# Gate products ahead of the value products, and the third half's q and k cast by GpSimd, in a fused attention and ReGLU kernel

## The chip, the cores and the metric

One core of a Trainium2 chip. The metric is the device time of one launch in microseconds (us); "before" is the kernel as it was, "changed" the kernel with the change. Runs of one kernel lie within 0.1 to 0.8% of each other; a step of 2 us between runs of the changed kernel's relatives is taken up in experiment 7.

## The reference, cut to what matters

```python
# attention: 4 batches, 8 heads, 768 positions, head dimension 64
scores = scale * q @ k.T + bias          # keep 8 global keys and a window of 96
a = softmax(scores); attn = a @ v
x = attn.transpose(0, 2, 1, 3).reshape(3072, 512)
# feed-forward: d_model 512, d_ff 1536
out = (relu(x @ w_gate) * (x @ w_val)) @ w_out      # float32
```

The kernel works on eight "halves" of 384 positions, two to a batch. Half s has its q and k transposed (head dimension onto partitions), its scores, exponentials and weighted sums made, and then goes through the feed-forward. Work of several halves is woven into one program for each engine. "Third half" below is s = 2, the first of the second batch.

## The kernel before: the parts that matter

The loads of q and k. The first half comes as fp32 on SyncE's queue; the second and third are cast to bf16 by the DMA on GpSimd's queue, in four pieces each:

```python
    def load_qk_cast(s, parts=2):

        b, half = divmod(s, 2)
        n = H // parts
        for i, (src, name) in enumerate(((q, "qs"), (k, "ks"))):
            t = stage.tile([128, H, NN * D], FP32, name=name)
            qk16[s, i] = t.rearrange("p h x -> p (h x)").bitcast(BF16).rearrange(
                "p (h x) -> p h x", h=H)[:, :, 0 : NN * D]
        for h in range(0, H, n):
            for i, src in ((1, k), (0, q)):
                nc.gpsimd.dma_start(
                    out=qk16[s, i][:, h : h + n],
                    in_=src[b, h : h + n, half * QH : (half + 1) * QH, :].rearrange(
                        "h (p n) d -> p h (n d)", n=NN))
```

The transposes on TensorE, and VectorE's copies out of PSUM, where the results of the matmuls lie. The DMA-cast halves are stored head by head, so each head has its own transpose of 64 columns:

```python
    def piece_t(s, p, pool=av_psum, name="av_ps"):
        tp = pool.tile([128, 512], FP32, name=name)
        tp = tp[:, 0:QH].bitcast(BF16).rearrange("d (i t) -> d i t", i=2)
        tp_of[s, p] = tp
        for i in (1, 0):
            for n in range(NN):
                for e in range(1 if s == 0 else 2):
                    r = slice(0, 128) if s == 0 else slice(64 * e, 64 * e + 64)
                    src = (cast_of[s, p][:, i, n] if s == 0
                           else qk16[s, i][:, 2 * p + e, n * D : (n + 1) * D])
                    nc.tensor.matmul(tp[r, i, n * 128 : (n + 1) * 128],
                                     lhsT=src, rhs=ident, is_transpose=True,
                                     start=(i == 1 and n == 0), stop=(i == 0 and n == NN - 1))

    def piece_copy(s, p):
        b, half = divmod(s, 2)
        tp = tp_of[s, p]
        put_keys(nc.vector.tensor_copy, nc.vector.tensor_copy, kT[b % 2][p], tp[:, 1, :], half)
        for e in range(2):
            r = slice(64 * e, 64 * e + 64)
            nc.vector.tensor_copy(qTb[s % 2][r, p, e, :], tp[r, 0, :])
```

The order of GpSimd's work and of the loads between the first and the third half. All of GpSimd's instructions and DMA issues run in this order:

```python
    for j in range(4, NT):
        load_v(0, j)
    load_w_group(1)
    load_w_group(2)
    load_qk_cast(2)
    load_w(wo_sb, moe_w_out, 0, DM)
# ... the second half and the first gate and value products ...
    for h in (0, 1, 6, 7):
        setup_mask(h)
    load_v_half(2)
    for p in range(HP):
        nc.gpsimd.memset(kT[1][p][:, 3, 32:128].bitcast(mybir.dt.uint32), 0)
        nc.gpsimd.memset(kT[1][p][:, 6, NG + 48 : 128].bitcast(mybir.dt.uint32), 0)
    nc.gpsimd.memset(vbuf[1][:, NT - 1, :].bitcast(mybir.dt.uint32), 0)
    for i in range(2):
        nc.gpsimd.memset(qz[i].rearrange("t n p e z -> t (n p e z)").bitcast(mybir.dt.uint32), 0)
    for j in range(NT):
        fill_ones(nc.gpsimd, 1, j)
    T2 = [(0.0, f) for p in range(HP) for f in (lambda p=p: piece_t(2, p, *QKB), lambda p=p: piece_copy(2, p))]
    weave(f1_1[G[0]] + f1_0[G[1]][4:] + f1_1[G[1]],
          [(0.05 + 0.06 * j, lambda j=j: fill_ones(nc.vector, 0, j)) for j in range(NT)],
          [(0.6, lambda: load_qk_after(3)), (0.6, lambda: load_v_half(3))],
          spread(T2, 0.55, 0.95))
```

`weave` places pieces of other work between the feed-forward products; `T2` is the list of the third half's transposes and copies, spread between 55% and 95% of that stretch.

`load_v_half(2)` puts three things in line: the load of the 8 global rows of v (GpSimd's queue), their spread to the other six v tiles of the batch by six small copies inside SBUF (SyncE's queue, which waits for that load), and the loads of four v tiles.

The softmax here doesn't subtract the row's maximum and nothing guards it: scores larger than these inputs give would overflow.

## Time and profile before

| | before |
|---|---|
| time, median | 253.31 us |
| span of the profiled run | 251.2 us |
| TensorE busy | 239.8 us (95%) |
| TensorE reaches the third half's transposes | 44.05 us |
| GpSimd's 13.78 us of idle time ends | 53.30 us |

TensorE is the bound. Times in timelines are from the span's start. A bracket at the end of a row is the idle time of that engine just before the row, and what ended it. PE is TensorE, DVE VectorE, ACT ScalarE, POOL GpSimd, SPq SyncE's queue, and L312 is line 312 of that kernel. qT and kT are the transposed q and k, xT is the attention's result transposed, ht the hidden values of the feed-forward. PEclk is the clock that TensorE was granted, as a share of full speed (in a page, in tenths). Only the stretch that the first part of the change aims at is shown here, from TensorE's timeline of the kernel before (start, length, line, operation):

```profile
19.41 0.34 PE L312 MATMUL qk_ps<-dd,sid 128*128 128x216 bf16 x2 [0.86 <-DVE qT L300]
...
20.27 0.36 PE L290 MATMUL ff_ps<-ident,ks 128*64 128x128 bf16 x6
```

The bias matmuls of the second half's first scores wait 0.86 us for VectorE's q copies.

### The profile page before, as it was taken

The numbers are of one execution on the slowest core, as the hardware profiler recorded it, in microseconds if no ns is written. First come the engines' busy times: TensorE is split into PE (matmuls) and PEld (weight loads), VectorE is DVE, ScalarE is ACT, GpSimd is POOL, SyncE is SP. The second block draws the span as 40 slices with busy tenths as digits, with TensorE's granted clock in tenths as the row PEclk, the third lists the DMA queues.
The fourth block names the chain that finished last, engine by engine and source line by source line (L and its number), as shares of the span: only waits on it lengthen the run. The fifth ranks groups of instructions, "written<-read, shape, count | busy, mean of one in ns | idle before, by whom it ended". The sixth has DMA issues, their size and how long they took to land.

```text
span 251.2 us, 4845 instructions
## 1 busy us (share of the span) xinstructions
PE 239.8 (95%) x1741; PEld 142.5 (57%) x1749; DVE 137.1 (55%) x352; ACT 156.8 (62%) x323; POOL 88.4 (35%) x205
## 2 busy tenths in 40 slices
PE   7679999999999999999999999999999999999993
PEld 4566665556454666556664666556655666556541
DVE  5959557966441467527662567527662557424410
ACT  7886874257654687557774687557774687553321
POOL 8996542059491067202527076203520000000000
PEclk9999999999999999999999999999999999999999
DMA  6999999959699666739468966738432100020012
GB/s 187 166 179 188 207 197 207 145 140 156 77 211 172 193 174 150 53 108 266 104 88 88 248 173 146 55 111 261 104 86 82 43 3 0 19 110 0 0 42 84
DMA packets 77431, 31.56 MB, mean 126 GB/s; under 512 B 57440, under 2 KB 74336, under 8 KB 77408
## 3 DMA queue, kind: packets, MB, share of 16 engines
q0 software_dynamic: 36080, 9.48, 37.1%
q1 hardware_dynamic: 41328, 21.78, 31.7%
q8 instruction: 13, 0.21, 0.4%
q14 instruction: 10, 0.08, 0.1%
HBM read 28.38 MB, written 6.29 MB: 138 GB/s over the span
## 4 chain that ended last, share of the span: by engine, by line
PE 83%; DVE 7%; ACT 6%; DMA 1%; issue 1%; SPq 1%; ACTq 0%
PE ff_ps L478 45%; PE ff_ps L501 24%; PE av_ps L410 5%; PE qk_ps L382 5%; DVE xT L427 2%; DMA qs<-in_q_dram 1%; DVE ht L494 1%; ACT es L335 1%; ACT grelu L487 1%; PE av_ps L441 1%; ACT rcp L424 1%; PE qk_ps L330 1%; ACT lnd L419 1%; DVE qT L300 1%; PE qk_ps L290 1%
## 5 line engine op out<-in xcount | busy, mean ns | idle before, releaser
L478 PE MATMUL ff_ps<-xT,wv 128*128 128x384 bf16 x384 | 78.1, 326 | 0.8 <-DVE ht L494 0.3
L478 PE MATMUL ff_ps<-xT,wg 128*128 128x384 bf16 x384 | 78.1, 326 | 0.0
L487 ACT ACTIVATE grelu<-ff_ps 128x384 bf16<-128x384 f32 x96 | 47.0, 490 | 33.7 <-PE ff_ps L478 13.5
L501 PE MATMUL ff_ps<-wo_sb,ht 128*128 128x512 bf16 x280 | 66.4, 379 | 0.4
L494 DVE TENSOR_TENSOR ht<-ff_ps,grelu 128x384 bf16<-128x384 f32 x96 | 53.2, 555 | 21.5 <-PE ff_ps L478 13.4
L427 DVE TENSOR_TENSOR xT<-av_ps,rcp 64x384 bf16<-64x384 f32 x48 | 26.6, 555 | 46.4 <-ACT rcp L424 41.9
L478 PEld LDWEIGHTS <-wv 128*128 128x128 bf16 x384 | 36.0, 97 | 23.4 <-issue 2.1
L478 PEld LDWEIGHTS <-wg 128*128 128x128 bf16 x384 | 36.0, 97 | 23.0 <-issue 0.2
L394 DVE TENSOR_TENSOR es<-es,m_all 128x432 bf16<-128x432 bf16 (+5 forms) x113 | 34.3, 332 | 26.0 <-ACT es L385 25.2
L385 ACT ACTIVATE es<-qk_ps 128x432 bf16<-128x432 f32 (+2 forms) x75 | 39.5, 529 | 9.4 <-PE qk_ps L382 7.7
L501 PEld LDWEIGHTS <-ht 128*128 128x128 bf16 x288 | 27.0, 97 | 28.3
L419 ACT ACTIVATE lnd<-av_ps 64x384 f32<-64x384 f32 x48 | 23.3, 485 | 13.3 <-PE av_ps L410 12.6
L506 ACT COPY osb<-ff_ps 128x512 f32<-128x512 f32 x24 | 14.1, 586 | 26.7 <-PE ff_ps L501 25.8
L338 POOL CAST kc<-ks 128x384 bf16<-128x384 f32 x20 | 10.0, 544 | 52.6 <-DMA ks<-in_k_dram 52.6
L382 PE MATMUL qk_ps<-qT,kT 128*128 128x432 bf16 (+5 forms) x113 | 25.8, 286 | 0.0
L151 POOL DMA_DIRECT2D vbuf<-in_v_dram x28 | 24.3, 874 | 3.8 <-DMA wg<-in_moe_w_gate_dram 2.4
L410 PEld LDWEIGHTS <-vbuf 128*128 128x128 bf16 x216 | 18.3, 98 | 8.7 <-issue 0.8
L410 PE MATMUL av_ps<-es,vbuf 128*128 128x216 bf16 (+4 forms) x216 | 21.4, 226 | 0.6 <-DVE xT L427 0.6
L382 PEld LDWEIGHTS <-kT 128*128 128x128 bf16 x113 | 10.9, 98 | 7.5
L346 POOL CAST qz<-qs 128x192 bf16<-128x192 f32 x40 | 12.4, 358 | 1.8 <-DMA qs<-in_q_dram 1.8
L424 ACT ACTIVATE rcp<-lnd 128x384 f32<-128x384 f32 x24 | 12.5, 523 | 0.8
L335 ACT ACTIVATE es<-qk_ps 128x432 bf16<-128x432 f32 (+2 forms) x15 | 7.0, 536 | 3.2 <-PE qk_ps L330 3.2
(92 smaller groups left out, 146.1 us busy)
## 6 DMA issues: line engine op xcount, KB each, us to landing
out_dram<-osb SPq DMA_DIRECT2D x24, 256.0 KB
ks<-in_k_dram SPq DMA_DIRECT2D x5, 768.0 KB
qs<-in_q_dram SPq DMA_DIRECT2D x5, 768.0 KB
vbuf<-in_v_dram POOLq DMA_DIRECT2D x24, 120.0 KB, 4.5
wg<-in_moe_w_gate_dram POOLq DMA_DIRECT2D x3, 512.0 KB, 9.1
wv<-in_moe_w_val_dram POOLq DMA_DIRECT2D x3, 512.0 KB, 10.9
wo_sb<-in_moe_w_out_dram POOLq DMA_DIRECT2D x1, 1536.0 KB, 19.1
ks<-in_k_dram SPq DMA_DIRECT2D x4, 192.0 KB
```

Source lines behind the costliest of these rows:

```text
L151: nc.gpsimd.dma_start(out=v_dst(b, NG + r0, NG + r0 + n, j), in_=v[b, :, KT * j + r0 : KT * j + r0 + n, :].rearrange("h p d -> p h d"))
L382: nc.tensor.matmul(ps[:, c : c + n_], lhsT=kt[:, j, :], rhs=qd[:, :, :, a : a + w], start=True, stop=True)
L385: nc.scalar.activation(es[:, 0:cols], ps[:, 0:cols], AF.Exp, bias=0.0, scale=scale)
L394: nc.vector.tensor_mul(e4, e4, mk)
L410: nc.tensor.matmul(av3[:, :, a : a + w], lhsT=vb[:, j, z0 : z0 + 128], rhs=es[:, c : c + NN * w].rearrange("k (n p) -> k n p", n=NN), star ...
L419: nc.scalar.activation(ln[o0 : o0 + 64], av[d0 : d0 + 64, 0:QH], AF.Ln, bias=0.0, scale=1.0)
L424: nc.scalar.activation(rc, ln, AF.Exp, bias=0.0, scale=-1.0)
L427: nc.vector.tensor_tensor(xT_of[s][r, p, :], av_of[s, p, e_][r, 0:QH], rc[r], op=ALU.mult)
L478: nc.tensor.matmul(st[key][:, 0:QH], lhsT=w_of(w, dc, fc), rhs=xT_of[c][:, dc, :], start=(dc == 0), stop=(dc == N_DC - 1))
L487: nc.scalar.activation(gr, psg[:, 0:QH], AF.Relu, bias=0.0, scale=1.0)
L494: nc.vector.tensor_tensor(ht[:, fc, :], psv[:, 0:QH], st["r", fc], op=ALU.mult)
L501: nc.tensor.matmul(ps2, lhsT=ht[:, fc, n * 128 : (n + 1) * 128], rhs=wo_sb[:, fc, :], start=(fc == 0), stop=(fc == N_FC - 1))
```

## The change

Its intent, as far as the diff shows it: (1) bring the first gate weights in before the second q/k half of the second half, and use them at once, so that TensorE has products to do while attention is short of work; (2) bring the third half's q and k in as fp32, let GpSimd cast them into the paired layout, and transpose 128 columns at once, which halves the number of transposes. A few setup tiles become bf16 to make room for a fourth gate buffer.

```diff
-    gr_pool = ctx.enter_context(tc.tile_pool(name="gr", bufs=3))
+    gr_pool = ctx.enter_context(tc.tile_pool(name="gr", bufs=4))
 ... load_qk takes the issuing engine, load_qk_cast a range of heads ...
-    gsrc = setupp.tile([NG, 2, NN, WQ], FP32)
-    gl = setupp.tile([NG, 2, NN, WQ], FP32)
+    gsrc = setupp.tile([NG, NN, WQ], BF16)
+    gl = setupp.tile([NG, 2, NN, WQ], BF16)
 ... in piece_t: two half-width transposes only for s == 1, else from cast_of ...
-    load_qk_cast(1)
-    load_w_group(0)
+    load_qk_cast(1, 0, H // 2)
+    load_w(wg[0], moe_w_gate, 0, GW * 128)
+    load_qk_cast(1, H // 2, H)
+    load_w(wv[0], moe_w_val, 0, GW * 128)
 ...
-    load_qk_cast(2)
+    load_qk(2, 0, H, nc.gpsimd)
     load_w(wo_sb, moe_w_out, 0, DM)
 ...
     S1(0)
+    gate, val = F0[0:8:2], F0[1:8:2]
+    gate[0]()
+    gate[1]()
+    gate[2]()
     copy_v_globals(V, 0, 4, NT)
 ... gate[3] follows the last transposes of the second half, then the value products ...
     for j in range(NT):
         fill_ones(nc.gpsimd, 1, j)
-    T2 = [(0.0, f) for p in range(HP) for f in (lambda p=p: piece_t(2, p, *QKB), lambda p=p: piece_copy(2, p))]
+    for p in range(HP):
+        cast(2, p, P, P)
+    T2 = [(0.0, lambda p=p: TC(2, p, *QKB)) for p in range(HP)]
```

More of the change, by code (lines that the diff above doesn't have):

```diff
@@ L103, with load_qk @@
     qs_of, ks_of = {}, {}
-    def load_qk(s, h0, h1):
+    def load_qk(s, h0, h1, eng=nc.sync):
         b, half = divmod(s, 2)
@@ L110, in load_qk @@
         for src, dst in ((k, ks_of[s]), (q, qs_of[s])):
-            nc.sync.dma_start(
+            eng.dma_start(
                 out=dst[:, h0:h1, :],
@@ L116, with load_qk_cast @@
     qk16 = {}
-    def load_qk_cast(s, parts=2):
+    def load_qk_cast(s, h0=0, h1=H):
         b, half = divmod(s, 2)
-        n = H // parts
-        for i, (src, name) in enumerate(((q, "qs"), (k, "ks"))):
-            t = stage.tile([128, H, NN * D], FP32, name=name)
-            qk16[s, i] = t.rearrange("p h x -> p (h x)").bitcast(BF16).rearrange(
-                "p (h x) -> p h x", h=H)[:, :, 0 : NN * D]
-        for h in range(0, H, n):
-            for i, src in ((1, k), (0, q)):
-                nc.gpsimd.dma_start(
-                    out=qk16[s, i][:, h : h + n],
-                    in_=src[b, h : h + n, half * QH : (half + 1) * QH, :].rearrange(
-                        "h (p n) d -> p h (n d)", n=NN))
+        for i, src, name in ((1, k, "ks"), (0, q, "qs")):
+            if (s, i) not in qk16:
+                t = stage.tile([128, H, NN * D], FP32, name=name)
+                qk16[s, i] = t.rearrange("p h x -> p (h x)").bitcast(BF16).rearrange(
+                    "p (h x) -> p h x", h=H)[:, :, 0 : NN * D]
+            nc.gpsimd.dma_start(
+                out=qk16[s, i][:, h0:h1],
+                in_=src[b, h0:h1, half * QH : (half + 1) * QH, :].rearrange(
+                    "h (p n) d -> p h (n d)", n=NN))
     def v_dst(b, r0, r1, j):
@@ L220 @@
     q1, q2 = [[1, NN], [NN, WQ]], [[0, 2], [-1, NN], [-NN, WQ]]
-    nc.gpsimd.affine_select(out=gl[:, 0], in_=gsrc[:, 0], compare_op=ALU.is_ge, fill=BIG,
+    nc.gpsimd.affine_select(out=gl[:, 0], in_=gsrc, compare_op=ALU.is_ge, fill=BIG,
                             base=-NL, pattern=q1, channel_multiplier=-1)
@@ L224 @@
                             base=0, pattern=q1, channel_multiplier=-1)
-    nc.gpsimd.affine_select(out=gl[:, 1], in_=gsrc[:, 1], compare_op=ALU.is_ge, fill=BIG,
+    nc.gpsimd.affine_select(out=gl[:, 1], in_=gsrc, compare_op=ALU.is_ge, fill=BIG,
                             base=-(NL - 1), pattern=q1, channel_multiplier=0)
@@ L285, in piece_t @@
             for n in range(NN):
-                for e in range(1 if s == 0 else 2):
-                    r = slice(0, 128) if s == 0 else slice(64 * e, 64 * e + 64)
-                    src = (cast_of[s, p][:, i, n] if s == 0
-                           else qk16[s, i][:, 2 * p + e, n * D : (n + 1) * D])
+                for e in range(2 if s == 1 else 1):
+                    r = slice(64 * e, 64 * e + 64) if s == 1 else slice(0, 128)
+                    src = (qk16[s, i][:, 2 * p + e, n * D : (n + 1) * D] if s == 1
+                           else cast_of[s, p][:, i, n])
                     nc.tensor.matmul(tp[r, i, n * 128 : (n + 1) * 128],
@@ L609, in S1, with TC @@
             piece_biased(1, p)
+    def TC(s, p, *pool):
+        piece_t(s, p, *pool)
+        piece_copy(s, p)
     piece_t(1, 0, *QKB)
@@ L617 @@
     S1(0)
+    gate, val = F0[0:8:2], F0[1:8:2]
+    gate[0]()
+    gate[1]()
+    gate[2]()
     copy_v_globals(V, 0, 4, NT)
-    piece_t(1, 2, *FFB)
+    S1(1)
+    piece_t(1, 2)
+    piece_t(1, 3)
     piece_copy(1, 2)
-    S1(1)
-    piece_t(1, 3, *FFB)
     piece_copy(1, 3)
-    F0[0]()
+    gate[3]()
     S1(2)
-    F0[1]()
-    F0[2]()
+    val[0]()
+    val[1]()
     AV(1, 0)
-    F0[3]()
     S1(3)
-    F0[4]()
-    F0[5]()
+    val[2]()
     AV(1, 1)
-    F0[6]()
+    val[3]()
     AV(1, 2, *QKB)
-    F0[7]()
     F0[8]()
```

## The prediction

> **What bounds the kernel now.** I read the page first, then the chain of waits, then the timelines of single engines where the change works.
>
> The page says that TensorE is the bound, and that its clock is full in every slice:
>
> ```profile
> PE 239.8 (95%) x1741; PEld 142.5 (57%) x1749; DVE 137.1 (55%) x352; ACT 156.8 (62%) x323; POOL 88.4 (35%) x205
> PE   7679999999999999999999999999999999999993
> PEclk9999999999999999999999999999999999999999
> ```
>
> Each digit is 6.28 us. Only the first three and the last are below 9. Of 251 - 240 = 11 us of TensorE idle about half lies before 20 us; the busy times by stretch give 1.52 us idle in 0 to 5, 1.61 in 5 to 10, 0.92 in 10 to 15, 1.45 in 15 to 20, 0.05 in 20 to 25, 0.16 in 30 to 40, none between 40 and 60, and 5.6 from there to the end, mostly the tail. Anything that makes TensorE wait after 25 us therefore adds its full length to the end, and anything saved before it counts only if no later wait swallows it. From the first transposes of the third half (seen next) TensorE has 251.2 - 44.05 = 207.15 us of nearly unbroken work.
>
> TensorE's timeline, start and length in us, around the third half's transposes (line 290):
>
> ```profile
> 43.30 0.81 PE L478 MATMUL ff_ps<-xT,wv 128*128 128x384 bf16 x4
> 44.05 0.36 PE L290 MATMUL qk_ps<-ident,ks 128*64 128x128 bf16 x6
> 44.24 0.33 PE L290 MATMUL qk_ps<-ident,qs 128*64 128x128 bf16 x6
> 44.51 0.82 PE L478 MATMUL ff_ps<-xT,wg 128*128 128x384 bf16 x4
> ```
>
> They read bf16 q and k that the DMA has cast on the way in, so no compute engine stands in front of them, and no bracket with a wait stands on the line. The change puts GpSimd there. So GpSimd's timeline is the one to read:
>
> ```profile
> 39.39 0.14 POOL L647 MEMSET kT<- 128x36 uint32 x1
> 53.30 0.55 POOL L648 MEMSET vbuf<- 128x544 uint32 x1 [13.78 <-DMA vbuf<-vbuf]
> 53.80 2.70 POOL L650 MEMSET qz<- 128x1536 uint32 x2
> 56.44 2.01 POOL L156 MEMSET vbuf<- 128x288 uint32 x7
> 58.40 2.43 POOL L151 DMA_DIRECT2D vbuf<-in_v_dram x3
> 60.82 1.85 POOL L338 CAST kc<-ks 128x384 bf16<-128x384 f32 x4
> ```
>
> GpSimd stands still for 13.78 us before the memset of line 648, which clears the last v tile of the second batch and overlaps a small copy of the global rows of v (vbuf to vbuf). It costs nothing now, because nobody needs GpSimd then. SyncE's timeline shows that copy and the wait table of its queue why it is late:
>
> ```profile
> 47.55 4.51 SPq L143 DMA_DIRECT2D vbuf<-vbuf  x6
> SPq L143 <- DMA vbuf<-in_v_dram: 42.7, 1, 42.7
> ```
>
> The copy waits for the load of those global rows, which is queued on GpSimd's DMA queue at 30.81, behind the output weights (1536 KB). The DMA engines are full from 2 to 47 us, so it lands at 47.55.
>
> **What the Trainium skill says.** (1) "TensorE: Matmul & The Clock Gate", the specification table at the head: ScalarE, VectorE and GpSimdE queues are 8 deep and strict FIFO. The trace agrees: GpSimd's starts above are in program order (lines 647, 648, 650, 156, 151, 338), with 13.78 us of idle in front of free work. (2) Same page, "What's actually happening": after an idle window of about 3.4 us the PE clock falls to half and needs about 3.4 us of activity to come back. The trace agrees in the start: seven warm-up matmuls of 128x512 take 3.17 us, 0.45 us each, while six of the same size of line 501 take 1.29 us in the chain of waits, 0.215 each. The granted clock reads 1.00 even there, so that row does not show it. (3) "DMA: Bandwidth & Descriptors", "Specifications": below 512 B the DMA does read-modify-write. The present cast loads write rows of 192 bf16, 384 B; fp32 rows are 768 B. (4) Same page, "Anatomy of one DMA": a wait on a semaphore happens on the issuing sequencer. The 42.7 us on SPq is such a wait.
>
> **The change part by part.**
>
> *First weights in two parts, gates first.* The first gate weights move ahead of the second q/k half of the second half; three gate products (3 x 4 matmuls, about 0.65 us each in a stream, so some 2 us) move to just after the first scores of the second half. TensorE is idle there: 0.86 us at 19.41 behind the qT copies, 0.42 at 17.23, 0.59 at 13.57. The products need only the first half's last xT (written 19.38 to 19.94) and the gate weights, which are now some 384 KB earlier in the queue (at about 200 GB/s, 2 us). Value weights keep their place (they land at about 24). I estimate 1 us saved up to 25 us, at most 1.5. The fourth gate buffer permits four gates ahead of the first value product and costs nothing.
>
> *Setup in bf16, smaller.* One memset of 0.42 us shrinks on VectorE, and GpSimd's selects keep their forms. The chain's start waits for q's DMA until 5.78. Zero.
>
> *Third half as fp32.* Two queue entries of 768 KB in place of four of 192 KB each... that is 1536 KB written in place of 768. From waits on DMAs eight back I read landings: last first-wave value weights about 35.8, output weights about 47.4; those are 1536 KB at the 205 GB/s of the weights, 7.5 us, so q and k took about 4.0. In fp32 the SyncE loads of the same size move at 358 to 373 GB/s alone (4.3 us) and at about 270 at the start (5.6 us). So the global rows land later by 0.3 to 1.6 us; I take +1.0.
>
> *Whole-width transposes.* Per pair of heads 6 transposes of 128 columns in place of 12 half-width ones. The twelve take 44.51 - 44.05 = 0.46 us; six 128-column ones at about 0.06 take about 0.36. Four pieces: -0.4 us.
>
> *Casts on GpSimd.* Eight casts of 128x384 fp32 to bf16; line 338 has the same shape: 4 in 1.85 us, 0.46 each. In program order they come **after** the memsets of lines 646 to 650 and the seven of line 156, so the first starts where now line 151 starts: 58.40, plus the 1.0 us of the later landing, 59.4. The first pair's k and q take 0.93: ready at 60.33, with some 0.05 until TensorE sees it, 60.4. TensorE arrives there at about 43 and, being in order with everything else queued behind, waits about 17 us. The shift of the rest is 60.4 - 44.05 = **+16.3 us**. The saving of the first part is inside that wait, so it is worth nothing. The later pairs come every 0.93 us, and TensorE does two products (1.3 us) between pieces: no further wait.
>
> *After the wait.* 17 us of idle make TensorE cold: some 3.4 us at half speed lose 1.7 us. The only later wait worth giving back is the 0.57 us before line 410 at 69.23: -0.6. GpSimd's preparation of the fourth half runs 4 to 5 us later, but TensorE needs it 16 us later.
>
> Sum: 253.3 + 16.3 + 1.7 - 0.6 - 0.4 = **270.3 us**, 6.7% slower.
>
> **The rivals.**
>
> *A, the intended gain.* If GpSimd's casts were done by 43 us, the time would be 253.3 - 1.0 - 0.4, about 252. This needs the casts ahead of the memset in GpSimd's order or the v copy to land 15 us earlier. Against: the text of the change puts the casts after the seven memsets, and nothing in it moves the copy, which hangs on a queue with full DMA engines (9 in every slice up to 47 us). At 252 it would read "same".
>
> *B, the wait is shorter.* fp32 rows of 768 B escape the read-modify-write, and two entries in place of four let the output weights be issued sooner. If the whole q/k load cost nothing, the global rows would land 4 us earlier, and the time would still be 265. Even then slower.
>
> *C, the wait is longer.* fp32 on this queue at the 205 GB/s of cast weights takes 7.5 us in place of 4: +3.5 in place of +1, and a cold clock over two windows another 1.7: about 274.5. The two are unlikely together.
>
> *D, moved bound.* GpSimd, with 3.7 us more work, delays the fourth half's q and k. It has 88 us of 251 busy and its fourth-half copies end at 72, while TensorE's clock of that stage moves by 16. Nothing.
>
> **Range and chances.** The core of the sum, +16.3, is two readings of the trace; the DMA shift (0.3 to 3.5) and the cold clock (0 to 3.4) carry the error: 267.0 to 273.5 for 8 in 10. Within the mechanism every case is far over 2% (258.4). I leave 7% for the order on GpSimd not being what I read: 0.02 faster, 0.05 same, 0.93 slower.
>
> **What would show it.** Right: GpSimd's memset of the last v tile with a wait of about 14 us on the v copy, casts from about 59.4, TensorE idle of 16 to 18 us in front of the third half's transposes, released by GpSimd's cast, and two to three slices of PE near 0; the first products after it at about double length; digits of 9 again to the end. Right on part one: TensorE reaches those transposes at about 43. Wrong: casts before 45 us, no such idle, a time near 252. A wait at the right place but with another length says that the DMA shift was mis-sized.

## The result, and the profile after

| | before | changed |
|---|---|---|
| time, median | 253.31 us | 270.65 us (270.35 to 271.44) |
| ratio, 95% interval | 1 | 1.0689 (1.0664 to 1.0714) |
| span of the profiled run | 251.2 us | 268.6 us |
| TensorE reaches the third half's transposes | 44.05 us | 44.0 us |
| TensorE starts them | 44.05 us | 59.52 us |

A ratio here is the mean time of one kernel's fast runs over the mean of the other's in the same rounds, so it is not quite the ratio of the medians.

In the page of the changed kernel each digit is a fortieth of the span, 6.7 us:

```profile
PE   7779995019999999999999999999999999999994
PEclk9999999556999999999999999999999999999999
```

There is one hole, two slices wide, and beside it a dip of the granted clock. To the right of them the row is as full as before. TensorE's timeline of the changed kernel at the hole (line 288 is the transpose, line 476 the products; in the kernel before they were 290 and 478):

```profile
43.28 0.81 PE L476 MATMUL ff_ps<-xT,wv 128*128 128x384 bf16 x4
59.52 0.95 PE L288 MATMUL qk_ps<-ident,qk 128*128 128x128 bf16 x6 [15.42 <-POOL qk L253]
60.26 1.49 PE L476 MATMUL ff_ps<-xT,wg 128*128 128x384 bf16 x4
...
65.36 0.50 PE L288 MATMUL qk_ps<-ident,qk 128*128 128x128 bf16 x6
```

The last four matmuls before the hole take 0.65 us in a stream, so TensorE is ready at about 44.0 (43.28 + 0.65 = 43.93). It stands for 15.42 us, released by GpSimd's cast (line 253). Four products then take 1.49 us where they took 0.82. GpSimd's timeline shows what the cast stood behind:

```profile
37.02 0.14 POOL L652 MEMSET kT<- 128x36 uint32 x1
53.87 0.55 POOL L653 MEMSET vbuf<- 128x544 uint32 x1 [16.71 <-DMA vbuf<-vbuf]
54.37 2.69 POOL L655 MEMSET qz<- 128x1536 uint32 x2
57.01 2.01 POOL L154 MEMSET vbuf<- 128x288 uint32 x7
58.97 0.49 POOL L253 CAST qk<-ks 128x384 bf16<-128x384 f32 x1
59.42 0.49 POOL L253 CAST qk<-qs 128x384 bf16<-128x384 f32 x1
```

And SyncE's timeline has the v copy 0.57 us later than before (47.55):

```profile
48.12 4.51 SPq L141 DMA_DIRECT2D vbuf<-vbuf  x6
```

The q that the cast reads had landed at 24.66 + 15.9 = 40.56 us (issue, and the longest time to landing of the qs loads of that queue). So the data waited more than 18 us for the engine, not the engine for the data.

For the first part of the change, the same place of TensorE's timeline as above, in the changed kernel:

```profile
19.44 0.34 PE L310 MATMUL qk_ps<-dd,sid 128*128 128x216 bf16 x2 [0.87 <-DVE qT L298]
...
20.21 2.11 PE L476 MATMUL ff_ps<-xT,wg 128*128 128x384 bf16 x12
```

The 0.87 us of waiting is still there, and the three gate products come after it.

### The profile page after: what moved, and what is told of

The parts are those of the page before. It is cut to its first block, busy times and chain, and to the rows that moved or that the text cites. A ratio compares the mean times of both kernels' runs of the same rounds, so it can differ in the third digit from the quotient of the medians.

```text
span 268.6 us, 4798 instructions
## 1 busy us (share of the span) xinstructions
PE 242.4 (90%) x1717; PEld 144.3 (54%) x1725; DVE 136.3 (51%) x352; ACT 156.6 (58%) x323; POOL 90.3 (34%) x211
## 4 chain that ended last, share of the span: by engine, by line
PE 69%; DMA 8%; issue 8%; POOL 6%; ACT 4%; DVE 4%; POOLq 0%; ACTq 0%; DVEq 0%
PE ff_ps L476 37%; PE ff_ps L499 23%; DMA wv<-in_moe_w_val_dram 8%; PE av_ps L408 4%; PE qk_ps L380 4%; DVE xT L425 2%; POOL vbuf L149 2%; DVE ht L492 1%; ACT rcp L422 1%; ACT lnd L417 1%; ACT grelu L485 1%; PE qk_ps L288 1%; POOL vbuf L154 1%; POOL ks L126 1%; POOL qz L655 1%
## 5 line engine op out<-in xcount | busy, mean ns | idle before, releaser
L476 PE MATMUL ff_ps<-xT,wg 128*128 128x384 bf16 x384 | 79.0, 330 | 0.0
L476 PEld LDWEIGHTS <-wg 128*128 128x128 bf16 x384 | 36.6, 99 | 23.1 <-issue 0.8
L392 DVE TENSOR_TENSOR es<-es,m_all 128x432 bf16<-128x432 bf16 (+5 forms) x113 | 33.2, 323 | 25.9 <-ACT es L383 25.2
L383 ACT ACTIVATE es<-qk_ps 128x432 bf16<-128x432 f32 (+2 forms) x75 | 39.4, 529 | 10.1 <-PE qk_ps L380 8.1
L288 PE MATMUL qk_ps<-ident,qk 128*128 128x128 bf16 x24 | 2.8, 264 | 15.4 <-POOL qk L253 15.4
L288 PEld LDWEIGHTS <-qk 128*128 128x128 bf16 x48 | 3.6, 112 | 17.1 <-POOL qk L253 16.0
```

The source lines that it names most:

```text
L383: nc.scalar.activation(es[:, 0:cols], ps[:, 0:cols], AF.Exp, bias=0.0, scale=scale)
L392: nc.vector.tensor_mul(e4, e4, mk)
L476: nc.tensor.matmul(st[key][:, 0:QH], lhsT=w_of(w, dc, fc), rhs=xT_of[c][:, dc, :], start=(dc == 0), stop=(dc == N_DC - 1))
```

## The experiments

Ten kernels ran, all with correct results. The theory at the start: what costs is the order on GpSimd, where the casts stand behind a memset that waits for the v copy. The rivals: the fp32 load or GpSimd's casts cost by themselves; the first part of the change saves something that the wait hides.

### 1. The casts ahead of the memsets

```diff
     load_v_half(2)
+    for p in range(HP):
+        cast(2, p, P, P)
     for p in range(HP):
         nc.gpsimd.memset(kT[1][p][:, 3, 32:128]...)
 ...
-    for p in range(HP):
-        cast(2, p, P, P)
```

> The changed kernel with GpSimd's eight casts of the third half moved ahead of its memsets, nothing else. Theory (the loss is only the order on GpSimd: the casts stand behind a memset that waits for the v copy): the casts start when k lands, about 38.5 us, and the first q about 40.7; the first pair is ready by 41.5, TensorE arrives at about 44 and waits for nothing; the time falls to 253.3 minus at most 0.4 for the fewer transposes, 252.9 us. Rival 1 (the fp32 load, the casts or GpSimd sharing with VectorE cost by themselves): 255 to 262, with a wait left in front of the transposes. Rival 2 (the first part of the change saved 1 us that the wait had swallowed): about 251.9.

Measured: 253.0 us, ratio to before 0.9981 (0.9954 to 1.0008). GpSimd's timeline:

```profile
38.75 0.50 POOL L253 CAST qk<-ks 128x384 bf16<-128x384 f32 x1 [1.86 <-DMA ks<-in_k_dram]
40.90 0.51 POOL L253 CAST qk<-qs 128x384 bf16<-128x384 f32 x1 [1.65 <-DMA qs<-in_q_dram]
```

and TensorE's:

```profile
44.02 0.50 PE L288 MATMUL qk_ps<-ident,qk 128*128 128x128 bf16 x6
44.35 0.81 PE L476 MATMUL ff_ps<-xT,wg 128*128 128x384 bf16 x4
```

The same eight casts of the same fp32 data, only earlier in one engine's order, and the 17 us are gone. The casts now wait for their loads, and no bracket stands on the transposes. This excludes the rival that fp32 or the casts cost by themselves. The six whole-width transposes take 0.33 us (44.35 - 44.02) in place of 0.46. Rival 2's 251.9 did not come either.

### 2. One memset moved, the casts left last

```diff
+    nc.gpsimd.memset(vbuf[1][:, NT - 1, :].bitcast(mybir.dt.uint32), 0)
     load_v_half(2)
 ...
-    nc.gpsimd.memset(vbuf[1][:, NT - 1, :].bitcast(mybir.dt.uint32), 0)
```

> The changed kernel with one line moved: GpSimd's memset of the last v tile of the second batch goes ahead of the loads of v, so that it waits for no copy; the casts stay last in GpSimd's order. Theory (what costs is the wait of that one memset): GpSimd runs through at 36 to 42 us, casts from about 42, the first pair ready at about 43; TensorE waits under 0.5 us; 252.9 to 253.5 us. If the length of GpSimd's queue ahead of the casts (5 us of memsets) and not the wait were the cost, about 5 us of the 17 would stay, 257 or more.

Measured: 268.03 us, ratio 1.0566 (1.0533 to 1.0599). A miss: I expected 253. GpSimd's timeline says why:

```profile
37.46 2.72 POOL L655 MEMSET qz<- 128x1536 uint32 x2
54.92 2.02 POOL L154 MEMSET vbuf<- 128x288 uint32 x7 [14.74 <-DMA vbuf<-vbuf]
56.89 0.50 POOL L253 CAST qk<-ks 128x384 bf16<-128x384 f32 x1
```

The seven memsets of ones into the same v buffer wait for the same copy. In the changed kernel that wait was hidden behind the first one: a trace shows only the first wait of a row of waits for the same thing. My theory that one memset was the cause falls. By the program text the ones and the copied rows lie in different columns of the tile, so no data is shared; that the wait comes from dependences kept for a coarser range than the columns written is my reading and was not tested. The memset of the last tile, by contrast, does overwrite eight rows that the copy wrote (the mask leaves those rows unused in that tile), so there the two cannot simply be taken as independent. What did help is that 0.55 and 2.7 us of work now ran before the wait. The copy itself came 0.9 us later in this run (49.01), so the casts start 2.1 us earlier (56.89 against 58.97), and the time is 2.6 us less. The remaining half microsecond is not explained.

### 3. The global rows of v queued ahead of the output weights

```diff
     load_qk(2, 0, H, nc.gpsimd)
+    load_v_globals(1)
     load_w(wo_sb, moe_w_out, 0, DM)
 ...
-    load_v_half(2)
+    spread_v_globals(1)
+    for j in range(4):
+        load_v(1, j)
```

> The changed kernel with the 8 KB load of v's global rows queued ahead of the output weights (1536 KB), nothing else moved. A dose: the rows should land about 7.5 us earlier (1536 KB at 205 GB/s), so the copy, the memset behind it, the casts and TensorE's restart each come 7.5 us earlier. Theory: restart at about 52.0 in place of 59.5, time 270.65 - 7.5 = 263.1 us. If another thing than this chain of waits set the restart, the time stays at 270 or moves by another amount.

Measured: two runs, 268.42 and 270.45 us, ratio 1.0626 (1.0571 to 1.0681). The size is a miss (263.1 expected). GpSimd's timeline:

```profile
49.99 0.55 POOL L656 MEMSET vbuf<- 128x544 uint32 x1 [12.59 <-DMA vbuf<-vbuf]
...
53.12 0.89 POOL L154 MEMSET vbuf<- 128x288 uint32 x3
56.13 1.17 POOL L154 MEMSET vbuf<- 128x288 uint32 x4 [2.12 <-DMA vbuf<-in_v_dram]
57.25 0.49 POOL L253 CAST qk<-ks 128x384 bf16<-128x384 f32 x1
```

The copy was issued at 40.56, 7.6 us earlier, as expected. But from issue to the end of the wait it took 9.4 us in place of 5.75, now beside the output weights on full DMA engines; that these slowed it was not tested. And the fourth memset of ones then waited for the load of its v tile, which is still behind the output weights. So the casts came only 1.7 us earlier. Again a second wait stood behind the first.

### 4. Both groups of memsets moved, the casts left last

```diff
+    nc.gpsimd.memset(vbuf[1][:, NT - 1, :].bitcast(mybir.dt.uint32), 0)
+    for j in range(NT):
+        fill_ones(nc.gpsimd, 1, j)
     load_v_half(2)
 ... both removed from their place after it ...
```

> The run with one memset moved showed that the next group on GpSimd, the seven memsets of ones into the same v buffer, inherits the wait for the v copy. Here both groups (the last tile's memset and the seven of ones) go ahead of the loads of v; the casts stay last on GpSimd. Theory as mended (every GpSimd write to that v buffer after the copy waits for it, and the casts stand behind them): no wait is left, the memset of qz runs at 37 to 40, the casts from 40 with the first q at about 41.2 when it lands, TensorE waits for nothing at 44, 252.9 to 253.3 us. Rival (casts or fp32 loads that cost by themselves, or yet another wait in GpSimd's order): 256 or more.

Measured: 252.97 us, ratio 0.9998 (0.9981 to 1.0016). GpSimd's timeline:

```profile
37.45 2.72 POOL L657 MEMSET qz<- 128x1536 uint32 x2
40.10 0.52 POOL L253 CAST qk<-ks 128x384 bf16<-128x384 f32 x1
40.55 0.51 POOL L253 CAST qk<-qs 128x384 bf16<-128x384 f32 x1
```

No wait is left and the loss is gone, with the casts still last in GpSimd's order. With experiment 1 this settles the cause as mended: GpSimd's writes to the v buffer after its loads, eight memsets in all, wait for the v copy or the v loads, and the casts stood behind them.

### 5. The first part alone

The changed kernel with the third half as in the kernel before (`load_qk_cast` in two parts, half-width transposes, no casts).

> The changed kernel with the third half as in the kernel before: cast by the DMA, half-width transposes, no casts on GpSimd. So the first part of the change alone, with the smaller setup and the fourth gate buffer. The prediction held that it saves 1 us (252.3), unseen behind the wait. The traces speak against it: TensorE reached the third half's transposes at about 44.0 in both kernels; the three gate products begin at 20.2, after the idle time that they were to fill (it ends at 19.44). So theory now: 253.2 plus or minus 0.3, nothing saved; rival: 252.3.

Measured: 253.32 us, ratio 0.9992 (0.9969 to 1.0015). It saves nothing that five rounds could see; the microsecond of the prediction is outside the interval (252.3 would be 0.996). In its profile TensorE reaches the third half's transposes at 44.13 us, against 44.05 before:

```profile
44.13 0.36 PE L288 MATMUL qk_ps<-ident,ks 128*64 128x128 bf16 x6
```

### 6. The third half's part alone

The kernel before with the fp32 loads, GpSimd's casts after its memsets, and whole-width transposes.

> The kernel before with the third half's part alone (fp32 loads on GpSimd's queue, casts on GpSimd after its memsets, whole-width transposes), without the first part. Theory: the whole loss is here, restart at about 59.5, 270.5 us, within 0.5 of the changed kernel. If the two parts added up in the time, it would differ from the changed kernel by what the first part gives (1 us by the prediction).

Measured: two runs, 269.18 and 271.18 us, ratio 1.0671 (1.0635 to 1.0706). All of the loss is in this part. In its profile TensorE restarts at 59.11:

```profile
59.11 0.95 PE L290 MATMUL qk_ps<-ident,qk 128*128 128x128 bf16 x6 [14.92 <-POOL qk L255]
```

### 7. TensorE kept warm through the wait

```diff
-    T2 = [(0.0, lambda p=p: TC(2, p, *QKB)) for p in range(HP)]
+    T2 = [(0.0, lambda p=p: (warm_up(68) if p == 0 else None, TC(2, p, *QKB))) for p in range(HP)]
```

> The changed kernel with 68 dummy matmuls of 128x512 (14.7 us at 0.216 each) put on TensorE directly ahead of the third half's first transposes, so that it is busy through the wait (15.4 us). Same result. Theory: the restart stays at 59.5, set by GpSimd's casts, but the clock is full there; the stretch from the first to the third piece of transposes, 5.84 us after the change against 3.72 before, returns to about 3.7; the time falls by 2.1 us to 268.5. If the slow products after the wait had another cause (GpSimd and VectorE sharing, the copies), the time stays at 270.6 or grows.

Measured: 269.30 us (269.09 to 269.59), ratio 1.0637 (1.0623 to 1.065). TensorE's timeline:

```profile
43.99 14.84 PE L240 MATMUL ff_ps<-warm 128*128 128x512 bf16 x68
59.64 0.79 PE L288 MATMUL qk_ps<-ident,qk 128*128 128x128 bf16 x6 [0.81 <-POOL qk L253]
60.27 0.81 PE L476 MATMUL ff_ps<-xT,wg 128*128 128x384 bf16 x4
...
66.95 0.81 PE L476 MATMUL ff_ps<-xT,wg 128*128 128x384 bf16 x4 [0.32 <-DVE ht L492]
```

The cause of the slow products was the clock: 0.81 us again. From the first to the third piece of transposes it is 63.20 - 59.64 = 3.56 us in place of 5.84, so the cold clock cost 2.28 us there. The whole fell by only 1.35 us (270.65 - 269.30): at full clock TensorE ran into two waits for VectorE's ht, 0.32 and 0.27 us, and it restarted 0.12 later. I had expected 2.1.

The clock in the changed kernel's own profile, by stretches (stretch, length, busy time and count of TensorE, weight loads, VectorE, ScalarE and GpSimd, then granted clock, DMA share, GB/s):

```profile
50.00:60.00 10.00, 0.48 (x4) 0.27 (x5) 0.00 (x0) 0.00 (x0) 6.13 (x13) 0.50 0.57 163
...
62.00:64.00 2.00, 2.00 (x12) 1.26 (x11) 0.85 (x2) 0.28 (x1) 2.00 (x4) 0.50 0.00 0
64.00:65.00 1.00, 1.00 (x5) 0.50 (x4) 0.99 (x5) 0.09 (x1) 1.00 (x2) 0.67 1.03 65
```

It is half until about 64.66 (a third of the slice from 64 to 65 at full clock gives 0.67), 5.1 us after the restart. In the profile of experiment 6 it is full again from about 62.0, 2.9 us after its restart.

Slices of 0.2 us show more. The clock was half from 47.60 to 64.67 in the changed kernel's profile, about 17.07 us long, and for about 13.65 us in those of experiments 2, 3 and 6: five and four times 3.41 us. Where the end of such a stretch falls decides how long TensorE works at half clock: 5.7, 3.1 and 2.9 us after the restart in experiments 2, 3 and 6.

The two lengths give mean clocks of 0.968 and 0.974, and the record has both: the runs of experiments 3 and 6 at 0.973 took 268.42 and 269.18, those at 0.968 took 270.45 and 271.18, and all four of the changed kernel were at 0.968. So the slower run of each pair fits one step of 3.41 us more at half clock, which costs at most 1.7 us of its 2.0. The slower runs have no profile, so this is not shown, and the rest stays open. What sets the steps was not tested. Experiment 7, whose clock stayed at 1.00, has a spread of 0.5 us.

### 8. Gate products put where TensorE does wait

Built on experiment 1. Three of the four matmuls of the first two gate products need only the first three pairs of heads; they go before the bias matmuls that wait.

```diff
 ... piece_bias takes a function and calls it ahead of its third bank ...
-    S1(0)
     gate, val = F0[0:8:2], F0[1:8:2]
-    gate[0]()
-    gate[1]()
+    piece_bias(1, 0, lambda: (gate[0](0, 3), gate[1](0, 3)))   # ahead of the third bank
+    piece_biased(1, 0)
+    gate[0](3, 4)
+    gate[1](3, 4)
     gate[2]()
 ...
     gate[3]()
+    val[0]()
     S1(2)
-    val[0]()
     val[1]()
```

> A try at a version better than both: the run with the casts first, and the gate products put where TensorE does idle. Three of the four matmuls of the first two gate products (those that need only the first three pairs of heads) go ahead of the third bank's bias matmuls, where TensorE waits 0.87 us for the qT copies; the first value product goes ahead of the third pair's scores, where it waits 0.33 us. Theory (a move pays only if its work is ready before the idle time ends): 253.0 - 0.8 - 0.3 = 251.9 us, ratio to before about 0.995. If the gate weights land too late (about 18.4 by the trace) or the DVE copies move too, 252.5 to 253.

Measured: 252.8 us, ratio 0.9983 (0.9967 to 0.9998). Less than expected. TensorE's timeline:

```profile
18.55 1.15 PE L478 MATMUL ff_ps<-xT,wg 128*128 128x384 bf16 x6 [0.19 <-DMA wg<-in_moe_w_gate_dram]
...
42.97 0.50 PE L288 MATMUL qk_ps<-ident,qk 128*128 128x128 bf16 x6
...
72.08 0.20 PE L382 MATMUL qk_ps<-qT,kT 128*128 128x48 bf16 x1 [0.72 <-POOL kT L273]
```

The products fill most of the idle time (0.19 us is left), and TensorE reaches the third half's transposes at 42.97 in place of 44.02: the whole expected microsecond. Then 0.72 us of it goes into a new wait for GpSimd's key copies of the fourth half. GpSimd's chain is still tied to the v copy, so it did not move when TensorE did.

### 9 and 10. Both together

Experiment 8 with the memsets moved as in experiment 4 (9), and besides with transposes and PSUM copies of the third half placed apart again as in the kernel before (10).

> The split gates reached the third half's transposes at 42.97 in place of 44.02 but gave the microsecond back: 0.7 us in a wait for GpSimd's key copies of the fourth half (GpSimd's chain was still held by the v copy until 54.2) and 0.7 in three waits for ht. Here the split gates are joined with GpSimd's v memsets ahead of the v loads. Theory: the wait for GpSimd's key copies goes, since its casts of the fourth half start 3 us earlier; 252.8 - 0.7 = 252.1 us, ratio about 0.995. If q and k of the fourth half (SyncE, behind the v copy) set the time of those copies, the wait stays and it is 252.8 again.

> As the combined run, and each piece's transposes and PSUM copies again placed apart, as in the kernel before. With them together VectorE's copies come in one block ahead of the products that need ht, and TensorE waits 0.7 us for ht in three places, where the kernel before waits 0.3. Theory: 0.3 to 0.4 us less than combined, 251.7 us, ratio 0.994. If the waits only move, no difference.

Measured: experiment 9 252.16 us, ratio 0.9956 (0.9941 to 0.9971), as expected. The wait for the key copies is gone from its table of waits: GpSimd casts the fourth half's k from 58.21 in place of 61.52, and waits there for the load of k, which stands behind the v copy in SyncE's queue:

```profile
58.21 1.97 POOL L338 CAST kc<-ks 128x384 bf16<-128x384 f32 x4 [9.39 <-DMA ks<-in_k_dram]
```

Experiment 10: 252.23 us, ratio 0.9964 (0.9944 to 0.9984); its waits for ht are 0.7 us in place of 0.6, so no gain, and my reason for it falls. Experiment 9 is faster than both kernels, by 0.4% against the kernel before, and the interval leaves out 1.

## Why the prediction was right

The time (270.3 predicted, 270.65 measured) and the mechanism held. The terms one by one:

| term of the sum | predicted | measured | from |
|---|---|---|---|
| later landing of v's global rows | +1.0 | +0.57 | the copy at 48.12 against 47.55 |
| restart of TensorE | 60.4 | 59.52 | timelines |
| shift of the rest | +16.3 | +15.47 | 59.52 - 44.05 |
| cold clock | +1.7 | about 2.3 | experiment 7, 5.84 - 3.56 |
| wait at line 410 given back | -0.6 | 0 | still 0.6 in the table of waits |
| whole-width transposes | -0.4 | -0.5 | 4 x (0.46 - 0.33) |
| whole, spans | +17.0 | +17.4 | 268.6 - 251.2 |

- **The wait on GpSimd** was at the place named, behind the v copy, with the casts from 58.97 (59.4 predicted). It was longer (16.71 against "about 14") because GpSimd reached it earlier, at 37 against 39.5, having issued its loads sooner. That has no bearing on the end.
- **The restart** was mis-sized by 0.9 us. 0.43 is the DMA term. The rest is that I let TensorE wait for both casts of the first pair. Its first three transposes need only k, and began when the k cast ended at 59.46.
- **The cold clock** was taken as one window of 3.4 us at half speed. It lasted 5.1 us in the profiled run, and between 2.9 and 5.7 us in four profiles (experiment 7). The loss was 0.6 us larger.
- **The wait at line 410** was expected to vanish once other work was late. It depends on ScalarE and VectorE work that moves along with TensorE, and it stayed.
- These errors are small and of both signs. The restart was put 0.9 us too late; the cold clock and the wait at line 410 cost 0.6 us more than put, each. That they nearly cancel, and leave 0.4 us, is luck.

Two things the prediction said beside the sum were wrong. First, **part one**: it said that TensorE would reach the transposes at about 43. It reached them at 44.0, and experiment 5 shows nothing saved. The step that failed is "TensorE is idle there": the products were put after the first scores, behind the very wait that they were to fill, and from there on the kernel before had hardly any idle time. The prediction's own line told against it: xT was written from 19.38 to 19.94, so no whole product could start before the 0.86 us of waiting ended at 19.41. Experiment 8 shows that the microsecond exists when the products stand ahead of the wait. Second, **one memset**: the prediction named the memset of line 648 as what the casts wait behind. Experiment 2 shows that the seven memsets behind it wait for the same copy. Rival A's way out ("the casts ahead of the memset") was right and gives 253.0, not 252, because part one is worth nothing.

## What to carry to other kernels

Before giving an engine work that others need, read that engine's own order, its harmless idle times above all: a wait that costs nothing today sets the start of everything placed behind it. When a wait is taken away, expect the next instruction to wait for the same thing; move the whole group or move the needed work ahead of it. Filling an idle gap needs the work ahead of the wait in program order and ready by then, and a gain on the bound engine lasts only as far as the engines that feed it are early too.

## What the Trainium skill lacked or had wrong

- "TensorE: Matmul & The Clock Gate", section "What you observe", has the full clock come about 4 us into sustained work, give or take 500 ns. After the long wait it came back 5.1 us after the restart in the changed kernel's profile, and 5.7, 3.1 and 2.9 us after it in those of experiments 2, 3 and 6, a wider spread than that section gives.
- "DMA: Bandwidth & Descriptors", section "Specifications", has a line-rate limit but no rate for loads that cast. In these runs 768 KB written by cast took about 4.0 us and 1536 KB of fp32 about 5.0 us (an estimate from the landings: a wait for the weights before it ends at 35.60, q lands at 40.56). Both read 1536 KB of fp32. The read-modify-write below 512 B, which the prediction took from that section, is not visible here: the cast load with its rows of 384 B was not the slower one. No run isolates it.
- No page says that a memset can wait for a DMA into other columns of the same buffer, as happened in experiment 2 (14.74 us). That the cause is how the program's dependences are kept was not tested.
